# One engine per PSUM tile, and edge rows kept from chunk to chunk, in a recurrent transformer kernel

## The chip, the cores and the metric

The kernel runs on one core of a Trainium2 chip. The metric is the device time of one execution in microseconds (us). Engines are named as in the profile: PE is TensorE (PEld its weight loads), DVE is VectorE, ACT is ScalarE, POOL is GpSimd, SP is SyncE, which only issues DMAs here.

## What is computed

Two different blocks, A and B, are applied to a sequence of 2048 rows of 640 numbers, twice over. A is attention over segments of 32 rows with a recurrent memory of 8 rows: the memory that a segment writes is what the next one reads. B is a mixer: layer norm, w1, GELU, a shift of four column groups by one or two rows up or down, w2, a residual, layer norm, w3, GELU, w4, a residual.

```python
def _A_ref(x, mem0, Wq, Wk, Wv, Wo, seg_len):     # 32 heads of 192, M = 8 memory rows
    mem = mem0
    for s in range(n_seg):                        # 64 segments of 32 rows
        h = concatenate([mem, x[segment s]], axis=1)
        q, k, v = h @ Wq, h @ Wk, h @ Wv
        p = softmax(where(mask, q k^T * scale, -1e9))
        o = (p v) @ Wo
        mem = o[:, :M]; outs.append(o[:, M:])

def _B_ref(x, w1, w2, w3, w4):
    h = gelu(layernorm(x) @ w1)
    g0, g1 = h shifted by one row down, up        # column groups of 160
    g2, g3 = h shifted by two rows down, up
    x1 = x + concatenate([g0, g1, g2, g3]) @ w2
    return x1 + gelu(layernorm(x1) @ w3) @ w4

x = x + A(layernorm(x)); x = x + B(layernorm(x))
x = x + A(layernorm(x)); x = x + B(layernorm(x))
```

## The kernel before

**Steps and lanes.** The memory makes A a chain of 64 segments. The two passes over the sequence are run as two lanes, the second five segments behind the first (`LAG`), so that a step handles 40 rows (8 of memory, 32 of the segment) of each lane, 80 columns in all. There are 69 steps, `attention_step(t)`; in the first five and the last five only one lane is at work (40 columns, widened to 56 in matmuls). Activations are held transposed: `hT` has the 640 features in five groups of 128 partitions and the 80 rows as columns.

**Within a step.** The 32 heads are taken in eight groups of four. For each group, K and Q are made with 30 matmuls each into the PSUM tiles `psk` and `psq` (line L943). `psk` is copied to `kT` in three pieces: one by VectorE (L962), and two of 64 partitions (`fk2`, L969) by the engines that `K_ON` names, ScalarE and VectorE. `psq` goes to `qT` by ScalarE (L954). V is made for two groups at once with narrow matmuls (L999). Then the scores `pss` (L1059), a masked minimum on VectorE (L1071), Exp on ScalarE (`Pm`, L1078), sum, reciprocal and product on VectorE (L1082 to L1084), a transpose of P (`pst`, L1094), its copy `PT` by ScalarE (L1102), and PV (`pso`, L1111). `pso` is copied to `oT` in two halves, `HALVES`: columns of the first three chunks of features by VectorE (L1124), the other three by ScalarE (L1122). Each half is what one of two blocks of 15 Wo matmuls waits for (`project`, L1146); they add up in `psy` over all eight groups.

**The turn of a step.** When `psy` is complete, its memory columns go to the next step's `hT` (`fm`, L1173): one lane's by ScalarE, the other's by VectorE. The segment's columns go to `yTB` (`fy`, L1181), where two steps of two lanes make a chunk of 64 rows per lane, interleaved, 128 columns. All K and Q matmuls of the next step need `hT`.

**Chunks.** Every second step a chunk of the mixer is started, `chunk(c)` and `chunk_end(c)`, whose operations are spread over the steps after it; there are 34. `yTB` is transposed into `psx` and added to the residual rows in `xw`; layer norm twice (for the residual and for B's own norm); the result is transposed back (`psv`) into `vT`; w1, GELU, w2, w3, GELU, w4 follow. As the shift needs two rows beyond the chunk, and the rows beyond are not there when the chunk is taken, a chunk's rows begin two before and end two before a multiple of 64. The kernel of before keeps four more columns in `yTB` (copied to its front by GpSimd, `fh`, L1354) and computes two rows per lane ahead: a second transposition `psl` of 68 columns (`ftl`, L1339), their residual rows by small DMAs (L1307) into `lnx`, an addition (`fl`, L1348), and a layer norm together with 64 rows of x that a later segment of lane 0 will need (`f1` to `f3`, L1375 to L1395), transposed together into `psvl`. At the chunk's end its output is normed and transposed (`psn`, 128 columns), and ScalarE copies every second column to the `hT` of lane 1 (L1669).

**Order.** The program writes no order by hand. Each `add(engine, cost, due, fn, r=, w=, ...)` gives a planner an operation with an estimated cost. The planner simulates the engines, PSUM slots (pools A with six banks, B with two) and the DMA rate, and at each point takes, among the operations that can start within about 0.1 us, the one with the lowest rank. `RANK` is a table of ranks per kind of operation, found by a search; a function that has no entry uses its due time. Engines execute in the order that the planner wrote. The planner knows reads and writes of tiles, but not that two engines that read one PSUM tile are put one behind the other in the built program. Costs are formulas such as

```python
def mm_us(n, m=128, k=1):
    return k * (max(54, n) / 2400.0 + 0.0025)
def dve_us(n, ps_=True):
    return ((120 if ps_ else 58) + n) / 960.0 + 0.02
def act_us(n, ps_=True):
    return ((172 if ps_ else 224) + n) / 1200.0 + 0.02
```

In the last chunk (`last`), which runs alone, `vT` is copied from `psv` in two parts by ScalarE and VectorE (`halves`, L1403 to L1411), and extra matmuls (`warm`, L1262) are inserted.

Of the kernel before, what the change touches and what calls it, by code (L numbers as in the profile page):

```python
# [9 lines left out]
ACT = mybir.ActivationFunctionType  # L10
# [19 lines left out]
K_ON = ("ACT", "DVE")  # L30
# [14 lines left out]
HALVES = tuple(range(8))  # L45
# [24 lines left out]
        "apply_ln.f": (52.137, 88.961, 100.699,),  # L70
        "chunk.f1": (110.438,),
        "chunk.f2": (101.84,),
        "chunk.f3": (65.664,),
        "chunk.fe": (83.886,),
        "chunk.fe3": (46.088,),
        "chunk.fel": (32.784,),
        "chunk.fh": (42.145,),
        "chunk.fhr": (183.031,),
        "chunk.fhs": (122.734,),
        "chunk.fl": (118.876,),  # L80
        "chunk.fs": (46.206, 100.871,),
        "chunk.ft": (77.438,),
        "chunk.ftl": (91.661,),
        "chunk.fw": (82.421, 86.103, 82.645, 37.823, 49.706, 86.304, 87.341, 97.836, 107.843, 101.597, 117.412,
            27.174, 138.348,),
        "chunk.fx": (144.278,),
        "chunk.fx0": (48.1, 109.648,),
        "chunk.fxu": (68.848,),
        "chunk.fz": (125.444,),
        "gelu.f1": (108.489, 105.663, 99.941, 44.304, 104.272, 85.543, 44.936,),  # L90
        "gelu.f2": (104.016, 80.087, 147.301, 105.313, 115.841, 68.271, 102.092,),
        "gelu.f3": (81.071, 47.257, 92.576, 102.866, 16.713, 80.182, 169.139,),
        "gelu.f4": (108.795, 187.178, 115.889, 52.134, 39.445, 121.226, 162.103,),
        "ln_ops.f1": (113.498, 100.865,),
        "ln_ops.f2": (188.826, 114.703,),
        "load_b.fn": (113.282, 90.237, 183.209, 88.687, 76.718, 75.796, -6.492, 37.287, 74.679, 84.079, 105.79,
            81.564, 80.465,),
        "transposes.f": (91.19, 65.988, 82.894,),
    },
    "chunk_end": {  # L100
        "apply_ln.f": (92.741,),
        "chunk_end.fc": (101.233, 116.192, 33.171,),
        "chunk_end.fs": (152.914, 113.991,),
        "chunk_end.fst": (127.26, 114.197,),
        "chunk_end.fw": (130.447, 151.132, 77.606, 37.432, 151.624, 84.736,),
        "chunk_loads.f": (118.19, 79.814, 119.586, 65.5, 181.368,),
        "chunk_loads.fz": (149.036, 115.195,),
        "ln_ops.f1": (113.153,),
        "ln_ops.f2": (114.194,),
        "load_b.fn": (25.784, 148.908, 91.004, 157.492, 132.751, 85.692,),  # L110
        "transposes.f": (110.897,),
    },
    "first": {
        "attention_step.attend.f1": (53.315, 116.534, 97.712, 137.116, 129.596, 117.185, 54.167, 51.79,),
        "attention_step.attend.f2": (122.453, 33.318, 74.77, 70.523, 95.566, 89.213, 89.302, 101.992,),
        "attention_step.attend.f3": (109.938, 136.679, 76.042, 26.902, 123.564, 59.921, 70.35, 117.182,),
        "attention_step.attend.f4": (113.68, 87.629, 101.379, 78.084, 61.992, 103.186, 162.766, 48.64,),
        "attention_step.attend.f5": (95.973, 87.397, 115.074, 90.598, 74.249, 85.169, 62.671, 71.515,),
        "attention_step.attend.f6": (74.769, 118.85, 101.445, 53.2, 100.179, 38.5, 91.303, 65.688,),
        "attention_step.attend.f7": (79.267, 98.733, 127.69, 88.769, 101.401, 86.207, 109.807, 86.175, 59.4,  # L120
            81.845, 106.636, 89.216, 138.087, 76.712, 83.255, 93.735,),
        "attention_step.attend.fs": (109.158, 111.417, 121.159, 106.123, 129.223, 60.084, 111.282, 89.653,),
        "attention_step.fm": (48.96,),
        "attention_step.fy": (147.298,),
        "attention_step.keys_queries.fk": (102.585, 78.188, 99.287, 130.281, 111.901, 98.238, 91.544, 26.406,),
        "attention_step.keys_queries.fk2": (84.393, 163.652, 93.092, 97.448, 123.943, 130.917, 84.608, 126.811,
            33.999, 145.838, 116.093, 88.348, 115.075, 53.318, 85.162, 95.305,),
        "attention_step.keys_queries.fn": (73.475, 112.773, 95.166, 81.821, 50.11, 70.037, 127.367, 101.817, 75.07,
            118.539, 89.588, 129.858, 81.31, 37.249, 94.633, 31.69, 99.13, 89.248, 36.06, 43, 122.012, 21.413,
            131.651, 100.541, 130.892, 45.487, 83.907, 168.92, 120.166, 121.565, 73.851, 39.608, 11.881, 106.339,  # L130
            115.663, 145.027, 152.756, 51.785, 45.777, 72.891, 99.831, 94.353, 134.505, 126.888, 62.508, 125.75,
            96.816, 104.126, 77.632, 95.91, 83.98, 53.33, 164.127, 50.166, 143.384, 116.988, 76.705, 99.607,
            33.732, 135.249, 118.307, 103.713, 122.872, 102.021,),
        "attention_step.keys_queries.fq": (145.726, 101.991, 16.584, 72.383, 49.052, 59.527, 124.407, 97.897,),
        "attention_step.project.f8": (88.21, 86.563, 74.946, 49.461, 60.12, 72.038, 18.799, 146.753, 47.648,
            103.867, 75.726, 33.177, 92.295, 61.69, 78.374, 47.025,),
        "attention_step.v_copy.fe": (163.555, 108.338, 123.289, 107.631, 99.982, 161.514, 102.494, 73.06, 78.25,
            18.618, 96.542, 112.184, 117.386, 89.453, 136.682, 217.373,),
        "attention_step.values.fv": (101.461, 63.658, 11.217, 34.926, 41.032, 75.23, -20.798, 105.83,),
        "load_pair.fn": (78.644, 162.287, 19.053, 53.265, -8.243, 105.654, 67.504, 48.03, 96.854, 77.189, 77.899,  # L140
            62.364, 106.57, 59.689, 7.158, 41.956, 127.74, 35.31, 53.318, 105.363, 82.67, 134.583, 66.545, 128.724,
            14.499, 15.468, 128.738, -7.887, 139.922, 75.799, 72.889, 115.019, 78.308, 62.361,),
        "res_tile.fn": (40.422, 9.668, 106.558, 121.267, 17.862, 103.756, 27.246, -8.673, 66.049, 57.216, 92.25,
            57.768, 102.896, 73.672, 49.835, 81.724, 97.237, 67.576, 68.752, 86.302,),
    },
    "last": {
        "apply_ln.f": (92.911, 107.765, 92.908,),
        "chunk.fc2": (102.878, 64.939,),
        "chunk.fhr": (130.275,),
        "chunk.fs": (89.257, 122.931,),  # L150
        "chunk.ft": (107.248,),
        "chunk.fw": (121.032, 126.614, 122.007, 82.468, 128.297, 91.565, 52.504, 72.633, 103.673, 132.715, 79.925,),
        "chunk.fx": (74.485,),
        "chunk.fxu": (116.946,),
        "chunk.fz0": (164.135,),
        "chunk.halves.fa": (16.494, 117.489,),
# [1615 lines left out]
```

## Time and profile before

| | |
|---|---|
| median of three runs | 3290.59 us (3289.48 to 3293.75) |
| profiled execution | 3296.21 us, its span 3294.5 us |
| granted TensorE clock, mean | 0.991 |
| TensorE busy | 3178.7 us (96%) |
| VectorE, ScalarE, GpSimd busy | 2361.9, 1908.4, 235.5 us |
| HBM | 250 GB/s over the span |
| ScalarE's and VectorE's copies of oT (552 each) | 189.6 us (mean 344 ns) and 214.0 us (388 ns) |
| VectorE's and ScalarE's small copies of kT (552 each) | 174.3 us (316 ns) and 152.2 us (276 ns) |
| ScalarE's copy qT (552) | 290.9 us (mean 527 ns) |

The span is the time from the first to the last instruction of the profiled execution; the execution's own time is 1.7 us more. A row of a group has its line, engine, operation, what is written and read with its form (partitions x elements), the count, and then the busy time and the mean. A row of waits names the engine, tile and line that waited, what ended the wait, and the time in total, the number of times and the longest. A row of the timeline has the start, the duration, the engine and line, and in brackets the idle time before and what ended it. A row of a stretch has the busy time of PE, PEld, DVE, ACT and POOL, the granted clock, the DMA share and GB/s.

### The profile page before, as it was taken

Reading aid. Unit: us, or ns where it says so; the run is one execution under the profiler, and the core shown is the slowest. Engines: PE = TensorE matmul, PEld = TensorE weight load, DVE = VectorE, ACT = ScalarE, POOL = GpSimd, SP = SyncE. Lnnn points to the kernel's source line nnn. Section 1 sums busy time; section 2 is a strip of 40 time slices with the busy share of each in tenths; the row PEclk is TensorE's granted clock in tenths of the full one; section 3 lists DMA queues with packets and bytes.
Section 4 is the critical chain, followed back from the end, with each engine's and each line's share of the span. In section 5 each row is a group of like instructions: output and inputs, shape, how many; then the busy total and the mean of one; then the engine's idle time right before and its main releaser. Section 6 shows DMA issues by size and latency. Waiting matters only on the chain.

```text
span 3294.5 us, 173909 instructions
## 1 busy us (share of the span) xinstructions
PE 3178.7 (96%) x77339; PEld 2809.6 (85%) x77341; DVE 2361.9 (72%) x7320; ACT 1908.4 (58%) x4837; POOL 235.5 (7%) x483
## 2 busy tenths in 40 slices
PE   5899999999999999999999999999999999999997
PEld 4788888888888888888888888888888888888876
DVE  2576777777777777777777777777777777777665
ACT  2346566666565656666666666565666666666443
POOL 0000000000000000000000000000000000000000
PEclk7999999999999999999999999999999999999999
DMA  9787778777777877777778777777877777777886
GB/s 372 249 285 260 236 245 272 239 237 249 265 239 235 271 245 237 240 265 252 238 245 274 234 232 256 261 237 237 276 243 235 241 268 244 237 251 264 271 282 203
DMA packets 409753, 833.67 MB, mean 253 GB/s; under 512 B 39680, under 2 KB 207311, under 8 KB 409000
## 3 DMA queue, kind: packets, MB, share of 16 engines
q1 hardware_dynamic: 401704, 809.47, 73.2%
q0 software_dynamic: 7136, 13.00, 1.3%
q8 instruction: 605, 9.91, 1.2%
q14 instruction: 148, 1.21, 0.1%
q10 hardware_dynamic: 160, 0.08, 0.0%
HBM read 817.14 MB, written 5.24 MB: 250 GB/s over the span
## 4 chain that ended last, share of the span: by engine, by line
PE 89%; DMA 3%; DVE 3%; ACT 3%; issue 1%; SPq 0%; POOL 0%; ACTq 0%; POOLq 0%; DVEq 0%
PE psy L1146 17%; PE psk L943 17%; PE psq L943 16%; PE psv L999 15%; PE pso L1111 5%; PE pss L1059 4%; PE psh L1565 3%; PE y L1611 3%; PE pst L1094 3%; PE psv L1039 2%; PE psh L1443 1%; DMA wst<-in_A_Wq_dram 1%; PE hs L1502 1%; DMA wst<-in_A_Wk_dram 1%; DVE oT L1124 1%
## 5 line engine op out<-in xcount | busy, mean ns | idle before, releaser
L943 PEld LDWEIGHTS <-wst 128*128 128x128 bf16 x19872 | 820.6, 99 | 51.9 <-issue 28.0
L1146 PE MATMUL psy<-oT,wo 128*128 128x80 bf16 (+1 forms) x16560 | 703.1, 200 | 30.5 <-DVE oT L1124 12.3
L979 ACT CAST V<-psv 96x384 bf16<-96x384 f32 (+3 forms) x1264 | 583.5, 473 | 195.2 <-PE psv L999 117.9
L1146 PEld LDWEIGHTS <-wo 128*128 128x128 bf16 x16560 | 637.8, 99 | 68.9 <-issue 50.6
L943 PE MATMUL psq<-hT,wst 128*128 128x80 bf16 (+1 forms) x9936 | 533.0, 200 | 7.9 <-DMA wst<-in_A_Wq_dram 4.8
L943 PE MATMUL psk<-hT,wst 128*128 128x80 bf16 (+1 forms) x9936 | 514.3, 200 | 19.7 <-DVE hT L1173 14.9
L999 PEld LDWEIGHTS <-hT 128*32 128x32 bf16 (+1 forms) x11840 | 294.7, 96 | 160.4 <-issue 8.6
L1124 DVE CAST oT<-pso 128x240 bf16<-128x240 f32 (+1 forms) x552 | 214.0, 388 | 280.9 <-ACT oT L1122 241.5
L954 ACT CAST qT<-psq 128x480 bf16<-128x480 f32 (+1 forms) x552 | 290.9, 527 | 101.6 <-PE psq L943 65.9
L999 PE MATMUL psv<-wv,hT 128*32 128x384 bf16 x5920 | 344.2, 328 | 0.1
L999 PE MATMUL psv<-wst,hT 128*32 128x384 bf16 x5920 | 341.6, 326 | 0.0
L1078 ACT ACTIVATE Pm<-pss,sm 80x320 bf16<-80x320 f32 (+2 forms) x552 | 278.1, 504 | 109.4 <-DVE sm L1071 101.3
L1071 DVE CUSTOM_DVE_ANT_1 pss<-pss,mask 80x320 f32<-80x320 f32 (+2 forms) x552 | 258.5, 468 | 114.3 <-PE pss L1059 104.6
L1102 ACT COPY PT<-pst 80x320 bf16<-80x320 bf16 (+2 forms) x552 | 221.9, 402 | 202.6 <-PE pst L1094 193.4
L969 ACT CAST kT<-psk 64x160 bf16<-64x160 f32 (+1 forms) x552 | 152.2, 276 | 310.0 <-PE psk L943 124.6
L943 PE MATMUL psq<-hT,wq 128*128 128x80 bf16 (+1 forms) x6624 | 322.0, 200 | 6.7 <-DMA wq<-in_A_Wq_dram 5.0
L943 PE MATMUL psk<-hT,wk 128*128 128x80 bf16 (+1 forms) x6624 | 321.4, 200 | 0.6 <-ACT hT L1698 0.4
L1122 ACT CAST oT<-pso 128x240 bf16<-128x240 f32 (+1 forms) x552 | 189.6, 344 | 219.0 <-PE pso L1111 169.2
L962 DVE CAST kT<-psk 128x320 bf16<-128x320 f32 (+1 forms) x552 | 256.1, 464 | 57.9 <-PE psk L943 20.8
L1082 DVE TENSOR_REDUCE sm<-Pm 80x4 f32<-80x320 bf16 (+2 forms) x552 | 250.4, 454 | 60.2 <-ACT Pm L1078 52.4
L943 PEld LDWEIGHTS <-wk 128*128 128x128 bf16 x6624 | 267.5, 99 | 11.8 <-issue 11.7
L1084 DVE TENSOR_TENSOR Pm<-Pm,sm 80x320 bf16<-80x320 bf16 (+2 forms) x552 | 255.7, 463 | 29.7 <-DVE sm L1083 0.5
(140 smaller groups left out, 4192.9 us busy)
## 6 DMA issues: line engine op xcount, KB each, us to landing
wst<-in_A_Wk_dram SPq DMA_DIRECT2D x556, 384.0 KB, 4.7
wst<-in_A_Wq_dram SPq DMA_DIRECT2D x556, 384.0 KB, 4.8
wst<-in_A_Wv_dram SPq DMA_DIRECT2D x418, 384.0 KB, 4.9
wstB<-in_B_w_dram SPq DMA_DIRECT2D x495, 320.0 KB, 4.6
wstB<-in_B_w_dram SPq DMA_DIRECT2D x132, 160.0 KB, 4.3
wo<-in_A_Wo_dram SPq DMA_DIRECT2D x8, 960.0 KB, 13.2
wv<-in_A_Wv_dram SPq DMA_DIRECT2D x2, 1536.0 KB
xw<-in_A_x_dram POOLq DMA_DIRECT2D x31, 80.0 KB, 4.6
```

The lines of the kernel that those rows point to most:

```text
L943: nc.tensor.matmul(out=o[:, cc, 0:W], lhsT=wv(kc, GW * j + cc * P, GW * j + (cc + 1) * P), rhs=h[:, kc, cw:cw + W], start=begin(pq), stop= ...
L954: nc.scalar.copy(out=qT[:, :, c0:c0 + N], in_=T(pq)[:, :, off:off + N])
L962: nc.vector.tensor_copy(out=k4[:, :, 0::3, c0:c0 + N], in_=p4[:, :, 0::2, off:off + N])
L979: (nc.vector.tensor_copy if e == "DVE" else nc.scalar.copy)(out=v_part(*dst), in_=a_)
L999: nc.tensor.matmul(out=o[32 * u:32 * u + n3, :], lhsT=left[:, kc, 32 * g3:32 * g3 + n3], rhs=wv(kc, a, a + GWH), start=(kc == 0), stop=(kc ...
L1071: nc.vector.tensor_tensor_reduce(out=o, in0=o, in1=maskt.unsqueeze(1).to_broadcast([NR, HG, N]), scale=-scale, scalar=3.0e38, op0=ALU.add, ...
L1078: nc.scalar.activation(out=Pb[0:NR, :, 0:N], in_=o, func=ACT.Exp, bias=sm_[0:NR, 0:1], scale=-1.0)
L1082: nc.vector.tensor_reduce(out=sm_[0:NR, 2:2 + HG], in_=Pb[0:NR, :, 0:N], axis=AX.X, op=ALU.add)
L1084: nc.vector.tensor_tensor(out=Pb[0:NR, :, 0:N], in0=Pb[0:NR, :, 0:N], in1=sm_[0:NR, 6:6 + HG].unsqueeze(2).to_broadcast([NR, HG, N]), op=A ...
L1102: nc.scalar.copy(out=Pt[0:KV, :, 0:N], in_=T(pst)[0:KV, :, c0:c0 + N])
L1124: nc.vector.tensor_copy(out=o_[:, 0:3, off:off + N], in_=T(pso)[:, 0:3, 0:N])
L1146: nc.tensor.matmul(out=o[:, m, cw:cw + W], lhsT=wo[:, cc, m * P:(m + 1) * P], rhs=o_[:, cc, 0:W], start=st, stop=True, skip_group_check=True)
```

## The change

Every PSUM tile is now read by one engine. `oT` is one copy of six chunks by ScalarE, which both Wo blocks wait for. The three pieces of `kT` are all VectorE's. The memory columns of both lanes are one VectorE copy. In the last chunk the transposes go to two tiles, of three and two groups, each with one engine.

The mixer's look-ahead is gone: no `psl`, `fl`, `fh`, no look-ahead rows in `lnx`. `yTB` has 128 columns; the two last rows of an odd step are written to its front, so a chunk's 128 columns are 62 of its own rows per lane and, in its first four columns, the two rows per lane that come after it. These serve as the two rows beyond (`vT`'s last four columns are copied from `psv`'s first four), and GpSimd keeps them in `edge_x` (rows 96 to 99 of the V tiles) for the next chunk, which puts them back as its first rows and norms them again with the statistics of the chunk before (`st4[0]` and `st4[4]` by turns). The loads of residual rows take two rows of the coming chunk per lane. The output's transposition is a matmul by every second column of the identity, into an f32 tile of 64 columns. `RANK` has new numbers throughout.

```diff
-K_ON = ("ACT", "DVE")
+K_ON = ("DVE", "DVE")
-HALVES = tuple(range(8))
 RANK = {
...
-    Vt = [ctile([KR, 2 * VP], bf16, f"V{i}") for i in range(VT_BUFS)]
+    Vt = [ctile([P, 2 * VP], bf16, f"V{i}") for i in range(VT_BUFS)]
...
-    yTB = ctile([P, KC, XB + 4], bf16, "yTB")
+    yTB = ctile([P, KC, XB], bf16, "yTB")
...
-    lnx = h2u[0:TOK + 4, Dm:2 * Dm]
+    lnx = h2u[0:TOK, Dm:2 * Dm]
...
+    edge_x = [v_[96:100, 0:Dm] for v_ in Vt]
...
-            if p_ in HALVES:
-                for hf in range(2):
-                    def f7(op, hf=hf):
-                        if hf:
-                            nc.scalar.copy(out=o_[:, 3:6, off:off + N], in_=T(pso)[:, 3:6, 0:N])
-                        else:
-                            nc.vector.tensor_copy(out=o_[:, 0:3, off:off + N], in_=T(pso)[:, 0:3, 0:N])
...
+            def f7(op):
+                nc.scalar.copy(out=o_[:, :, off:off + N], in_=T(pso)[:, :, 0:N])
+            add("ACT", act_us(GC * N), hi - HI[0], f7, r=(pso,), w=(ok,))
...
-                add("PE", mm_us(W, k=3 * KC), due, f8, r=(wb, oks[hf]), a=(psy,), order=order)
+                add("PE", mm_us(W, k=3 * KC), due, f8, r=(wb, ok), a=(psy,), order=order)
...
-            for e_, l in zip(("ACT", "DVE"), take):
...
+        if len(take) == 2:
+            def fm(op):
+                v = hn[:, :, SEG:SEG + 2 * M].rearrange("p k (l m) -> p k l m", l=2)
+                o = T(psy)[:, :, SEG:SEG + 2 * M].rearrange("p k (l m) -> p k l m", l=2)
+                nc.vector.tensor_copy(out=v[:, :, ::-1, :], in_=o)
+            add("DVE", dve_us(2 * KC * M), due, fm, r=(psy,), w=[B("hT", (t + 1) % 4, "m", l) for l in take])
...
+                nc.vector.tensor_copy(out=yv[:, :, l if t < T_A - 1 else 0, t0:t0 + n0], in_=T(psy)[:, :, xc:xc + n0])
+                if n0 < SEG:
+                    nc.vector.tensor_copy(out=yv[:, :, l if t < T_A - 2 else 0, 0:2], in_=T(psy)[:, :, xc + n0:xc + SEG])
...
+            if not last and 0 <= w0 + TOK <= S - 2:
+                todo.append((lane, lane, w0 + TOK, 2))
...
-        if not last:
-            add("PE", mm_us(128, k=KC), D(0.06), ftl, r=(B("yTB", 0), B("yTB", 1)), w=(psl,))
...
-        if not last:
-            add("DVE", 0.48, D(0.06), fl, r=(psl,), w=(B("lnx", "l"),))
...
-        if not last:
-            add("POOL", 0.7, D(0.1), fh, r=(B("yTB", 1),), w=(B("yTB", "h"),))
...
+        own, other = (0, 4) if c % 2 == 0 else (4, 0)
...
+            def fk0(op):
+                nc.gpsimd.tensor_copy(out=edge_x[c % 2], in_=xw[0:4, :])
+            add("POOL", 1.2, D(0.08), fk0, r=(xk,), w=(B("edge", c % 2),))
...
+            def fk1(op):
+                nc.gpsimd.tensor_copy(out=xw[0:4, :], in_=edge_x[1 - c % 2])
+            add("POOL", 1.2, D(0.15), fk1, r=(B("edge", 1 - c % 2),), w=(xk,))
+            apply_ln(uw, xw, 4, st4[other], 0, uk, xk, B("st", other), D(0.16))
...
-            nc.scalar.copy(out=vT[:, :, XB:XB + 4], in_=T(psl2)[:, :, TOK:TOK + 4])
+            nc.scalar.copy(out=vT[:, :, XB:XB + 4], in_=T(ps2)[:, :, 0:4])
...
-            ps4 = ps(PB, [P, KC, XB], bf16, "psn")
-            transposes(ps4, vx2, XB, D(1.5), (vxk,))
+            ps4 = ps(PB, [P, KC, TOK], f32, "psn")
+
+            def ft4(op):
+                for m in range(KC):
+                    nc.tensor.matmul(out=T(ps4)[:, m, :], lhsT=vx2[:, m * P:(m + 1) * P], rhs=ident[:, 0::2],
+                                     start=(m == 0), stop=(m == KC - 1), skip_group_check=True)
+            add("PE", mm_us(TOK, k=KC), D(1.5), ft4, r=(vxk,), w=(ps4,))
...
-                nc.scalar.copy(out=hT[tt % 4][:, :, d0:d0 + b - a], in_=pv[:, :, 0, a:b])
+                nc.scalar.copy(out=hT[tt % 4][:, :, d0:d0 + b - a], in_=T(ps4)[:, :, a:b])
```

## Prediction

> **What bounds the kernel now.** I read the page's first lines first, then the busy time of a long stretch, then who waits for whom, and last the timeline around single waits.
>
> ```profile
> PE 3178.7 (96%) x77339; PEld 2809.6 (85%) x77341; DVE 2361.9 (72%) x7320; ACT 1908.4 (58%) x4837; POOL 235.5 (7%) x483
> ...
> PEclk7999999999999999999999999999999999999999
> ```
>
> TensorE is the bound: the clock is full after the first slice, and no other engine reaches 75%. The stretch from 300 to 3000 us is the steady part:
>
> ```profile
> 300.00:3000.00 2700.00, 2662.46 (x64648) 2372.57 (x64646) 2009.37 (x6139) 1655.17 (x4086) 196.80 (x397) 1.00 0.75 249
> ```
>
> 98.6% looks as if nothing were left, but a matmul's row lasts 0.2 us while the next one is issued long before: in the timeline 18 matmuls of 80 columns take 0.81 us and 6 take 0.38, so one is issued every 0.036 us. A pause of up to some 0.16 us in the issue is therefore covered by the row before it, and every idle time shown is some 0.16 us too short. So I counted. In this stretch the groups have 13596 matmuls for Wo and 27293 for Q and K at 0.036 us, 11380 narrow ones for V at 0.041 (16 in 0.83 us, 4 in 0.34), 2724 for the scores (a third of them with 160 columns, at 0.07), 5428 for the transposes of P and for PV at 0.036, 2405 for the mixer's wide ones at 0.056, 962 at 0.136, and 860 transposes, mostly at 0.056. The sum is about 2562 us. So about 138 of 2700 us (5%) is lost in the issue, not 38. Two kinds of saving exist: fewer matmuls, and shorter pauses.
>
> Who makes TensorE pause, and who makes the copying engines pause:
>
> ```profile
> PE psk L943 <- DVE hT L1173: 14.9, 29, 0.5
> PE psy L1146 <- DVE oT L1124: 12.3, 64, 0.7
> ...
> PE pso L1111 <- ACT PT L1102: 7.0, 39, 0.4
> ...
> PE pss L1059 <- DVE kT L962: 5.0, 6, 1.3
> ```
>
> ```profile
> DVE oT L1124 <- ACT oT L1122: 241.5, 234, 2.2
> ...
> DVE kT L969 <- ACT kT L969: 69.5, 134, 2.6
> ...
> DVE hT L1173 <- ACT hT L1173: 51.2, 58, 1.3
> ```
>
> The second list is the finding: wherever one PSUM tile is emptied by both engines, the second copy waits for the first. The split costs time instead of saving it, and 362 us of VectorE's queue stand still behind it. The timeline shows it for the output of a head group, and at the turn of a step:
>
> ```profile
> 1505.52 0.36 ACT L1122 CAST oT<-pso 128x240 bf16<-128x240 f32 x1 [1.05 <-PE pso L1111]
> ...
> 1505.91 0.41 DVE L1124 CAST oT<-pso 128x240 bf16<-128x240 f32 x1 [0.57 <-ACT oT L1122]
> ...
> 1537.04 0.19 ACT L1173 CAST hT<-psy 128x40 bf16<-128x40 f32 x1 [1.32 <-PE psy L1146]
> 1537.26 0.20 DVE L1173 CAST hT<-psy 128x40 bf16<-128x40 f32 x1 [1.11 <-ACT hT L1173]
> ...
> 1537.52 0.81 PE L943 MATMUL psk<-hT,wst 128*128 128x80 bf16 x18 [0.52 <-DVE hT L1173]
> ```
>
> **The change part by part.** The sum is made against the profiled execution, 3296.2 us (span 3294.5, and 1.7 around it); the median of the three runs, 3290.6, lies 5.6 lower.
>
> *Fewer matmuls.* The look-ahead transposes psl go: five in each of 33 chunks.
>
> ```profile
> 1539.51 0.45 PE L1339 MATMUL psl<-ident,yTB 128*68 128x128 bf16 x5
> ...
> 1539.79 0.38 PE L943 MATMUL psk<-hT,wst 128*128 128x80 bf16 x6
> ```
>
> The next group starts 0.28 us after them, so 33 x 0.28 = 9.2 us of pure issue. The five psn transposes of a chunk (0.28 us too) become matmuls with 64 moving columns, every second one of the identity; by the 80-column row (0.036) and the 68-column psvl I take 0.03 each, 0.15 a set, so 33 x 0.13 = 4.3 us. No row shows a moving operand read with a step; if it ran at half rate this saving would be 0, and I see no reason for a loss beyond that. The psvl set runs in 30 chunks instead of 33: 0.5 us. Sum 14.0, range 9.5 to 14. It is real time, since TensorE is the bound.
>
> *The turn of a step.* The next step's first K matmul waits for two copies in a row, 1537.04 to 1537.46. One VectorE copy of 128x80 takes their place; between its rows of 128x40 (0.200) and 128x160 (yTB, 0.342) that is about 0.25 us. So 0.17 us less at each of the 58 turns with two lanes, 9.9 us; only 29 of the waits are visible, which gives 4.9 as the low end. I take 8. The copy must find VectorE free: behind an operation of 0.49 us it would lose what it gains, and it has no second engine to fall back on; hence a low end of 0.
>
> *oT by ScalarE alone.* Before, 0.36 and 0.41 us one behind the other, 0.79 from the first start to the last end. After, one copy of 480 elements: the qT row has the same form (mean 0.527, 0.55 with two lanes). A group's whole output is ready 0.24 us earlier, its first half 0.14 to 0.19 later. Here the Trainium skill speaks against the change: TensorEngine Tiling (Array Packing), section PSUM Bottleneck, advises using ScalarE and VectorE both to empty PSUM. By that rule the halves would be done together in 0.41 us and the change would cost 0.14 x 552 groups = 77 us of latency. The trace says otherwise: the second half waits 241.5 us for the first engine, and another page, PSUM — Partial Sum Buffer, section on bank collisions, says why one would order them so: two engines reading one bank in the same partitions at once is an error that the hardware does not arbitrate. I go by the trace. TensorE's waits for VectorE's oT are 12.3 us in 64 times, with 0.16 for each 22.5. The first Wo block of a group now starts later than the first half allowed, so I take half, 12 us, with ends of 0 and 22.
>
> *kT by VectorE alone.* 0.49, 0.33 and 0.33 us on one queue, 1.15 us against 0.49, 0.28 and 0.33 with two hand-overs, about the same. Q's 30 matmuls (1.08 us) lie between K and the scores and hide it; TensorE waited six times in all. Taken as 0; without that cover 0.1 us x 552 = 55 us either way, which nothing in the trace suggests.
>
> *Load of the copying engines.* VectorE loses 214 us (oT), gains 552 x 0.316 = 174 (kT), loses fl's 16, gains 33 applications on four rows (0.44 each, 15) and the strips of the last two rows of yTB (64 x 0.17, 11): about 30 less. ScalarE gains 290 - 190 = 100 (oT) and loses 152 (kT) and 13 (hT): 65 less. More counts that VectorE no longer stands still for ScalarE 362 us, nor ScalarE for VectorE 118 (87.1 on kT, 30.5 on oT), with softmax steps queued behind. What TensorE waits for there is PT, 7.0 us in 39 times, with 0.16 each 13.2, and Pm, 2.8 us in five times: I take a third of the 17, 6 us, ends 0 and 12. ScalarE's queue has a longer piece now: a PT copy (0.40) or Exp that comes just after an oT copy starts waits up to 0.19 us more.
>
> *Mixer edges.* GpSimd gets two copies of 4x640 per chunk (fk0, fk1) and loses fh (128x20, 0.19) and the look-ahead loads; it issues five loads a chunk as before, since two-row loads now go into xw. They wait, as the main ones, for the last reader of xw (row L1626). The loads of L1307, ahead of which GpSimd stood 1288 us, are gone; nobody waited for those. No row shows the copy; the memset of 4x640 took 0.62 us, the planner charges 1.2. The power operation of the layer norm can be queued behind fk0, and the row-4 application waits for fk1, but uw is needed only after w1, the GELU and w2. A second rule bears on this: SBUF — State Buffer, section on the two separate sides, says that GpSimd and VectorE share a port pair, held for a whole instruction against VectorE operations in a two-port mode or with two SBUF inputs. By it 66 copies of 0.62 to 1.2 us could hold VectorE up by 41 to 79 us; no row here shows such a delay. VectorE is idle a quarter of the time, so I take 0 for TensorE and keep 20 us (0.6 a chunk, if each hit a turn or a softmax) as the far end.
>
> *Tail and one-lane steps.* At 3268.4 ScalarE 0.48, VectorE 0.29 and ScalarE 0.18 run in a row before psh; from two banks they run side by side, 0.65 instead of 1.12, and a part of it again at 3281: 0.6 us. The one-lane steps from 3072 on lose 4 us each of 48 even in the visible rows; shorter chains may give 2.
>
> *New order.* Every due rank is changed, so which block fills which pause is drawn anew. That can't be costed; it counts in both directions in the range.
>
> Sum: 14 + 8 + 12 + 6 + 2.6 = 42.6. 3296.2 - 42.6 = 3253.6 for a profiled execution, 3248 for the median.
>
> **The rivals.** (A) *Only the work counts*: pauses are moved, not shortened, because TensorE then waits for PT or Pm instead. For it: softmax is a chain over ScalarE and VectorE with every link already in the list of waits. Against: the turn of the step has nothing behind it but that copy. 14 + 2 us: 3275. (B) *Slower, by the late first half*: the order puts Wo close behind PV, and TensorE waits for ScalarE's one long copy, 0.14 us beyond what the first half allowed before. With turn, work and tail still gaining 24.6, this decides from 24.6 / 0.14 = 176 of the 552 groups on; with 350 of them it is 49 us, so 3315. Against: before, with a latency of 0.79, only some 71 visible waits of 552 were for oT. (C) *More is won*: an order found with copies that take what the planner thinks (it planned both halves at once) halves the 138 us: 69 + 14 + 3 = 86, so 3205. (D) The edit turns out empty, for example because all was hidden: 3290; the psl rows make this unlikely.
>
> **How the numbers follow.** About 0.2% (6.6 us) is what a measurement can tell from no change. Forecast 0.45, own range 3228 to 3272; A 0.22; C 0.14; B 0.15; D 0.04. Faster 0.45 + 0.22 + 0.14 less a little of A's edge: 0.80; same 0.05; slower 0.15. The range leaves out B and the lower part of C: 3200 to 3288.
>
> **What would show it.** After: no psl rows and psn at half its issue; no wait of a copy for the other engine's copy of the same tile; psk waiting about 0.35 instead of 0.52 at a turn; fewer waits of psy for oT; VectorE some 30 and ScalarE some 65 us less busy. More than 150 psy waits for ScalarE's oT would show B; new PT and Pm waits of the old total A. A longer span with fewer pauses at turns would make the account by steps wrong and point to the order.

## The result, and the profile after

The changed kernel takes 3265.19 us (median of four runs) against 3292.17 for the kernel before in the same set: a ratio of 0.9912, 95% interval 0.9888 to 0.9936. In a second set, with more runs of before beside it, the ratio was 0.9913 (0.9897 to 0.9930), 3263.21 against 3293.58. So the change is worth 27 to 30 us, 0.9% (the intervals reach from 21 to 37 us). The forecast was 42.6 us less, 3248; the measured time lies inside the stated range.

The page's engine line and the granted clock, and a stretch of the steady part (busy PE, PEld, DVE, ACT, POOL, clock, DMA share, GB/s):

```profile
PE 3149.0 (96%) x77161; PEld 2790.2 (85%) x77161; DVE 2285.5 (70%) x7377; ACT 1854.6 (57%) x4217; POOL 269.6 (8%) x510
...
PEclk8999999999999999999999999999999999999999
```

```profile
300.00:2970.00 2670.00, 2638.09 (x64463) 2357.43 (x64466) 1939.93 (x6181) 1610.89 (x3570) 227.84 (x424) 1.00 0.75 251
```

TensorE is still the bound, at 98.8% of the stretch by its rows and a full clock. It has 178 matmuls fewer than before. By this line VectorE has 76 us less to do and ScalarE 54 (30 and 65 were expected), GpSimd 34 more. The line counts rows that overlap once; with all durations added up, VectorE has 33 us less, near the expected 30, and ScalarE 58. TensorE's waits now (in total, times, longest):

```profile
PE psx L1202 <- DVE vbg L1192: 9.7, 1, 9.7
PE psk L928 <- DVE hT L1149: 9.6, 29, 0.3
...
PE psq L928 <- DMA wst<-in_A_Wq_dram: 8.6, 16, 1.1
...
PE pst L1079 <- DVE Pm L1069: 5.2, 7, 1.5
...
PE psy L1122 <- ACT oT L1104: 4.3, 11, 0.5
...
PE pso L1096 <- ACT PT L1087: 3.1, 11, 0.5
...
PE pss L1044 <- DVE kT L947: 1.7, 3, 0.9
```

The turn of the step fell from 14.9 to 9.6 us, oT from 13.9 (12.3 for VectorE's half, 1.6 for ScalarE's) to 4.3, PT from 7.0 to 3.1. What came in their place stands in the same list: weights that land late, 8.6 us in 16 times against 4.8 in 8, and Pm, 5.2 against 2.8. The first row is one wait in the first 15 us of the run; it was 3.4 us before. The list of VectorE's waits has no copy of an oT, kT or hT tile by ScalarE any more; its longest is the wait for TensorE itself (`DVE hT L1149 <- PE psy L1122`, 160.0 us). A turn in the timeline (start, duration, engine, line), with one copy in place of two in a row:

```profile
1529.10 0.24 DVE L1149 CAST hT<-psy 128x80 bf16<-128x80 f32 x1 [3.83 <-PE psy L1122]
...
1529.39 1.02 PE L928 MATMUL psk<-hT,wst 128*128 128x80 bf16 x24 [0.33 <-DVE hT L1149]
```

The wait is 0.33 us where it was 0.52. From step 6 to step 63 only every second turn looks like this. At the others a block of the mixer stands between Wo and K, here in the kernel before, so that no idle time shows:

```profile
1586.48 0.72 PE L1565 MATMUL psh<-hTB,wstB 128*128 128x128 bf16 x10
1587.16 1.02 PE L943 MATMUL psk<-hT,wst 128*128 128x80 bf16 x24
```

The output's transposition with the stepped identity:

```profile
1517.20 0.31 PE L1631 MATMUL psn<-ident,h2u 128*128 128x64 bf16 x5
1517.35 0.38 PE L928 MATMUL psk<-hT,wst 128*128 128x80 bf16 x6
```

The next group starts 0.15 us after it, so a moving operand read with a step of two is issued at the full rate, 0.03 us for 64 columns.

One delay is new. GpSimd's copies of the edge rows hold up VectorE's `stash` copy (rows of V put by for later, bf16, from SBUF to SBUF) when the two meet:

```profile
310.99 0.71 POOL L1351 COPY xw<-V 4x640 bf16<-4x640 bf16 x1 [2.95 <-DVE h2u L1192]
...
311.15 0.82 DVE L1007 COPY stash<-V 32x384 bf16<-32x384 bf16 x2 [0.30 <-ACT V L964]
```

The first of these two VectorE copies took 0.65 us, ending 0.11 us after GpSimd's. In the profile 29 of the 464 `stash` copies meet a copy into `xw`, and these 29 took 0.66 us each where the others took 0.25: 12 us in all. No engine is listed as waiting for them.

**An account of TensorE's issue.** Matmul rows hide short pauses, as the prediction says, so I made the same sum for every run: from the first matmul of a group to the first of the next, less the group's issue time (columns / 2.4 ns and 2.5 ns for each matmul, as in the planner's formula, which gives the 0.036 us of the rows for 80 columns; 0.040 us for a narrow V matmul), where more than 0.06 us is left, put down to what released it. It is taken from the first K matmul of step 6 to that of step 63, the part with two lanes. "Switch" is the time lost on going into the narrow V matmuls and out of them. Going in costs 0.096 us. Going out shows as 0.14 or 0.15 us, but four narrow matmuls follow four others by 0.1625 us and not by 0.160; with that, 0.106 us remain, and 46 of the 55.8 us. Each row is one profile. The two profiles of the changed kernel (after, after2) differ by 6.3 us in length, so differences of a few us between two lengths tell nothing by themselves.

| us, in the stretch | length | switch | oT | turn | PT | Pm | kT | weights |
|---|---|---|---|---|---|---|---|---|
| before | 2713.0 | 55.8 | 28.8 | 22.5 | 12.2 | 3.4 | - | 3.0 |
| b_oT | 2709.0 | 55.7 | 26.0 | 22.5 | 17.4 | 0.5 | - | 5.7 |
| b_turn | 2708.6 | 56.4 | 28.9 | 13.9 | 11.3 | 2.8 | - | 2.2 |
| b_copies | 2695.4 | 53.5 | 28.5 | 13.9 | 1.1 | 10.0 | - | 3.1 |
| b_pework | 2703.0 | 55.3 | 29.1 | 22.5 | 12.2 | 2.8 | - | 2.3 |
| b_all | 2683.4 | 52.7 | 28.5 | 13.9 | - | 5.1 | 9.6 | 3.4 |
| after | 2684.3 | 58.8 | 11.2 | 13.9 | 6.8 | 0.8 | - | 13.6 |
| after2 | 2678.0 | 61.5 | 11.2 | 13.9 | 6.8 | 0.3 | - | 7.7 |
| a_split | 2738.2 | 53.3 | 44.4 | 13.9 | 19.5 | 2.9 | 23.9 | 4.9 |

The whole gain of the profiled pair lies in this stretch, 28.7 us: 12.2 us less issue time (2572.3 and 2560.1) and 16.5 us less lost (140.7 and 124.2). The start, up to step 6, is 1.4 us longer than before, and the end from step 63 on is as long (279.7 and 279.5 us).

### The profile page after: what moved, and what is told of

Same layout as the page of the kernel before. It is cut to its first block, busy times and chain, and to the rows that moved or that the text cites. A ratio compares the mean times of both kernels' runs of the same rounds, so it can differ in the third digit from the quotient of the medians.

```text
span 3266.9 us, 172868 instructions
## 1 busy us (share of the span) xinstructions
PE 3149.0 (96%) x77161; PEld 2790.2 (85%) x77161; DVE 2285.5 (70%) x7377; ACT 1854.6 (57%) x4217; POOL 269.6 (8%) x510
## 4 chain that ended last, share of the span: by engine, by line
PE 88%; DMA 7%; issue 2%; DVE 2%; ACT 1%; SPq 0%; POOL 0%; POOLq 0%; ACTq 0%; DVEq 0%
PE psq L928 16%; PE psy L1122 16%; PE psk L928 16%; PE psv L984 15%; PE pss L1044 5%; PE pso L1096 5%; PE psh L1531 3%; DMA wst<-in_A_Wq_dram 3%; PE y L1577 3%; PE pst L1079 2%; DMA wst<-in_A_Wk_dram 2%; PE psv L1024 2%; PE psh L1409 1%; PE hs L1468 1%; DMA wst<-in_A_Wv_dram 1%
## 5 line engine op out<-in xcount | busy, mean ns | idle before, releaser
L928 PEld LDWEIGHTS <-wst 128*128 128x128 bf16 x19872 | 803.7, 99 | 64.1 <-issue 35.7
L1122 PE MATMUL psy<-oT,wo 128*128 128x80 bf16 (+1 forms) x16560 | 703.6, 200 | 26.4 <-issue 8.6
L964 ACT CAST V<-psv 96x384 bf16<-96x384 f32 (+3 forms) x1264 | 595.9, 474 | 168.3 <-PE psv L984 102.4
L1122 PEld LDWEIGHTS <-wo 128*128 128x128 bf16 x16560 | 630.8, 99 | 51.2 <-issue 35.1
L928 PE MATMUL psq<-hT,wst 128*128 128x80 bf16 (+1 forms) x9936 | 518.0, 200 | 13.7 <-DMA wst<-in_A_Wq_dram 8.6
L928 PE MATMUL psk<-hT,wst 128*128 128x80 bf16 (+1 forms) x9936 | 508.6, 200 | 17.7 <-DVE hT L1149 9.6
L1104 ACT CAST oT<-pso 128x480 bf16<-128x480 f32 (+1 forms) x552 | 293.7, 532 | 264.0 <-PE pso L1096 238.9
L954 DVE CAST kT<-psk 64x160 bf16<-64x160 f32 (+1 forms) x1104 | 340.4, 308 | 131.3 <-PE psk L928 62.6
L984 PE MATMUL psv<-wst,hT 128*32 128x384 bf16 (+1 forms) x5920 | 343.3, 326 | 2.2 <-issue 1.1
L928 PEld LDWEIGHTS <-wk 128*128 128x128 bf16 x6624 | 270.8, 99 | 17.6 <-issue 13.9
L928 PEld LDWEIGHTS <-wq 128*128 128x128 bf16 x6624 | 267.4, 99 | 6.5 <-DMA wq<-in_A_Wq_dram 3.0
## 6 DMA issues: line engine op xcount, KB each, us to landing
wo<-in_A_Wo_dram SPq DMA_DIRECT2D x8, 960.0 KB, 12.3
```

What stands on the lines that cost most here:

```text
L928: nc.tensor.matmul(out=o[:, cc, 0:W], lhsT=wv(kc, GW * j + cc * P, GW * j + (cc + 1) * P), rhs=h[:, kc, cw:cw + W], start=begin(pq), stop= ...
L954: copy(out=k4[r0:r1, :, jj, c0:c0 + N], in_=p4[r0:r1, :, 1, off:off + N])
L964: (nc.vector.tensor_copy if e == "DVE" else nc.scalar.copy)(out=v_part(*dst), in_=a_)
L984: nc.tensor.matmul(out=o[32 * u:32 * u + n3, :], lhsT=left[:, kc, 32 * g3:32 * g3 + n3], rhs=wv(kc, a, a + GWH), start=(kc == 0), stop=(kc ...
L1104: nc.scalar.copy(out=o_[:, :, off:off + N], in_=T(pso)[:, :, 0:N])
L1122: nc.tensor.matmul(out=o[:, m, cw:cw + W], lhsT=wo[:, cc, m * P:(m + 1) * P], rhs=o_[:, cc, 0:W], start=st, stop=True, skip_group_check=True)
```

## The experiments

The theories: (1) a PSUM tile that two engines empty makes TensorE pause, and issue time is real time, so the parts have their worth in any order and add up; (2) what a part is worth is decided by the order around it; (3) two engines empty a tile faster than one. All edits but those of the ranks keep each engine's order of instructions; only the edited ones differ. Ratios are to the kernel before, timed beside them.

**b_oT**: oT whole by ScalarE, in the kernel before.

```diff
+                both_ = []
...
-                        if hf:
-                            nc.scalar.copy(out=o_[:, 3:6, off:off + N], in_=T(pso)[:, 3:6, 0:N])
-                        else:
-                            nc.vector.tensor_copy(out=o_[:, 0:3, off:off + N], in_=T(pso)[:, 0:3, 0:N])
+                        if not both_:
+                            nc.scalar.copy(out=o_[:, :, off:off + N], in_=T(pso)[:, :, 0:N])
+                        both_.append(op)
```

> The kernel before, in its own order of instructions on every engine, with one edit: each oT tile is copied whole by ScalarE (at the place of the first of its two half copies), VectorE's half is gone. Theory 1 (a PSUM tile emptied by two engines makes TensorE pause, whatever the order): 12 to 18 us less than before, TensorE's waits for oT fall from 14 us to under 7, and VectorE's wait for ScalarE's oT copy (241.5 us) is gone. Theory 2 (the gain comes from the new order, the old order has the pauses built in): under 4 us less, the waits for PT or Pm grow by what those for oT lose. Theory 3 (two engines are better than one): slower by up to 20 us, more psy waits for ScalarE's oT.

Measured: 3287.63 against 3290.82, ratio 0.9991 (0.9980 to 1.0002). The waits of TensorE in its profile:

```profile
PE pso L1111 <- ACT PT L1102: 10.3, 58, 0.4
...
PE psy L1146 <- ACT oT L1123: 5.3, 15, 1.0
```

The visible waits for oT fall from 13.9 us to 5.3, but in the account they are 26.0 us in 168 times where there were 28.8 in 139: short waits, since the first Wo block now needs the whole copy. And PT comes later, behind the longer copy on ScalarE's queue: 10.3 us visible against 7.0. Where a PT copy comes just after an oT copy, it starts more than 0.1 us after its transposes have ended in 69 of 138 cases, before in 8 of 109. Theory 1 had its 12 to 18 us here and got at most 6.6 (the interval's end). It fails for this part, in this order; theory 3 fails too. What theory 2 said (under 4 us, PT later) is what came.

**b_turn**: one VectorE copy for the memory columns of both lanes, in the kernel before.

```diff
+            both_ = []
...
+                    if len(take) == 2:
+                        if not both_:
...
+                            nc.vector.tensor_copy(out=v[:, :, ::-1, :], in_=o)
+                        both_.append(op)
+                        return
```

> The kernel before, in its own order, with one edit: at a turn with two lanes the memory columns of both lanes are copied by one VectorE instruction instead of ScalarE and then VectorE. Theory 1: 8 to 10 us less; the visible wait at a turn falls from 0.52 us to about 0.33. Theory 2: under 3 us. Theory 3: no gain, since VectorE comes late to it (slower by up to 5 us).

Measured: 3284.13 against 3290.82, ratio 0.9977 (0.9969 to 0.9986), 4.6 to 10.2 us. The wait at the turn:

```profile
PE psk L943 <- DVE hT L1177: 9.6, 29, 0.3
```

It was 14.9, 29, 0.5. Theory 1 holds for the wait itself: the account's turn goes from 22.5 to 13.9 us. At 28 turns with nothing between Wo and K, 0.68 us of lost issue becomes 0.50; at 29 with a block of the mixer between, 0.12 us becomes nothing. How much of the 8.6 us the kernel gets is less sure. By the medians it is 6.7; the stretch is 4.4 us shorter, as waits before Q and K matmuls grew by 4, which is within what two profiles of one kernel differ by.

**b_copies**: both of these, and all pieces of kT by VectorE.

```diff
-copy = nc.vector.tensor_copy if K_ON[jj - 1] == "DVE" else nc.scalar.copy
+copy = nc.vector.tensor_copy
```

> The kernel before, in its own order, with all three copy edits: oT whole by ScalarE, memory columns of both lanes in one VectorE copy, all three pieces of kT by VectorE. Theory 1: the two gains add up, 20 to 28 us less, kT adding nothing. Theory 2: under 7 us less. If kT counts, this lies more than 5 us away from the sum of the other two runs.

Measured: 3278.11 against 3290.82, ratio 0.9961 (0.9949 to 0.9974), 12.7 us. That lies between what theories 1 and 2 allowed (20 to 28, under 7). The sum of the two runs before is 9.9, so kT's part is 2.8 by the medians; by the stretch it is 9.2 (17.7 against 4.1 and 4.4). No run has the kT edit alone, so its part stays open. By the account PT's waits are gone (1.1 us of 12.2) and Pm's have come up (10.0 of 3.4): taking ScalarE out of kT helps ScalarE's softmax step and hurts VectorE's.

**b_pework**: less work for TensorE, copies split as before. VectorE's addition after psl is left out too (not shown), so the look-ahead rows lack the attention's output.

```diff
-            for m in range(KC):
-                nc.tensor.transpose(out=o[0:TOK + 4, m, :], in_=yTB[:, m, XB - TOK:XB + 4], identity=ident[:, :])
...
-            transposes(ps4, vx2, XB, D(1.5), (vxk,))
...
+                for m in range(KC):
+                    nc.tensor.matmul(out=T(ps4)[:, m, :], lhsT=vx2[:, m * P:(m + 1) * P], rhs=ident[:, 0::2],
+                                     start=(m == 0), stop=(m == KC - 1), skip_group_check=True)
```

> The kernel before, in its own order, with only TensorE's work cut: the look-ahead transposes psl and the addition after them are left out (so the look-ahead rows lack the attention's output), and the output's transposition has 64 moving columns, every second one of the identity, instead of 128. The copies stay split over two engines. Theory 1 (issue time is real time): 13.5 us less, of which 9.2 from psl and 4.3 from the 64 columns; the next group starts 0.15 us after the first psn matmul instead of 0.28. Theory 2 (pauses absorb it): under 5 us less. If the stepped operand is read at half rate: 9 us less and psn still takes 0.28.

Measured: 3284.04 against 3290.82, ratio 0.9983 (0.9972 to 0.9993), so 2 to 9 us, less than expected. In the steady stretch, with 29 of the 33 chunks, it is 10.1 us shorter, of 11.9 that 0.41 us a chunk would give. The two readings don't agree, so the cost was put to the test the other way round.

**b_psl4**: every psl transpose four times.

```diff
-            for m in range(KC):
+            for m in [m_ for m_ in range(KC) for _ in range(4)]:
                 nc.tensor.transpose(out=o[0:TOK + 4, m, :]
```

> The kernel before, in its own order, with every psl transpose issued four times instead of once: 15 more matmuls of 128 columns in each of 33 chunks, at 0.056 us 27.7 us in all. Theory 1 (issue time is real time): 24 to 30 us slower than before, so that psl itself was worth 8 to 10. Theory 2 (pauses absorb half of it, as the 6.8 us for an expected 13.5 of the run with the cut work suggest): 10 to 18 us slower.

Measured: 3317.54 against 3293.01, 24.5 us more, ratio 1.0079 (1.0054 to 1.0103). One block in the timeline:

```profile
1549.83 1.28 PE L1339 MATMUL psl<-ident,yTB 128*68 128x128 bf16 x20
1550.94 0.38 PE L943 MATMUL psk<-hT,wst 128*128 128x80 bf16 x6
```

1.11 us to the next group, four times 0.28. The steady stretch is 23.0 us longer, of 24.4 for 29 chunks. So some nine tenths of issue time is run time (the interval allows 18 to 34 us of the 27.7); by this, psl is worth 8 us or a little more, and the cut work as a whole, as an estimate, some 12. Theory 1 holds for TensorE's work. Why b_pework got less, with an interval that ends at 9 us, is not explained.

**b_all**: b_copies and b_pework together, in the order of the kernel before (the edits are those of the runs before). The changed kernel's copies and second norms of the edge rows and its last chunk are not in it.

> The kernel before, in its own order, with the three copy edits and the cut TensorE work together (psl and the addition after it left out, so the look-ahead rows lack the attention's output; psn with 64 columns). Apart from the order and the edge rows' bookkeeping this is the changed kernel. Copies alone gave 12.7 us and the cut work 6.8 by the medians. Theory 1 (parts add, the new order is worth nothing by itself): 24 to 29 us less than before, level with the changed kernel within 4 us. Theory 2 (the order has to be searched for whole copies): 17 to 21 us less, 6 to 10 us behind the changed kernel, with psy's waits for ScalarE's oT still above 25 us in all.

Measured: 3267.14 against 3293.58, 26.4 us less, ratio 0.9924 (0.9909 to 0.9938). It is level with the changed kernel, 3.9 us behind by the medians of the same set, with overlapping intervals. The single parts by medians add up to 12.7 + 6.8 = 19.5, by the steady stretch to 17.7 + 10.1 = 27.8 (b_all: 29.6). Theory 1 holds for the whole: these edits without a new order give nearly all of the gain.

**after2**: the changed kernel in the same set.

> The changed kernel once more, on the same chip as the others of this set: 25 to 31 us less than before.

Measured: 3263.21, 30.4 us less. In the account the new order has 17 us less in waits for oT than b_all (11.2 and 28.5) and none for kT, but more at switches, in waits for PT and for weights. It exchanges waits; the net of order and edge rows together is those 4 us or nothing.

**a_split**: oT in two halves again, in the changed kernel and its order.

```diff
-                nc.scalar.copy(out=o_[:, :, off:off + N], in_=T(pso)[:, :, 0:N])
+                nc.vector.tensor_copy(out=o_[:, 0:3, off:off + N], in_=T(pso)[:, 0:3, 0:N])
+                nc.scalar.copy(out=o_[:, 3:6, off:off + N], in_=T(pso)[:, 3:6, 0:N])
```

> The changed kernel, its order kept, with one edit: at the place of ScalarE's whole oT copy, VectorE copies the first half and ScalarE the second. Theory 1: the second copy waits for the first, the output is ready some 0.25 us later and both Wo blocks wait for it: 8 to 20 us slower than the changed kernel, VectorE's and ScalarE's waits for each other's oT come back. Theory 2 (in any order other work covers it): within 4 us of the changed kernel.

Measured: 3332.13, 68.9 us more than the changed kernel of the same set and 38.6 more than before (ratio to before 1.0118, 1.0103 to 1.0133). ScalarE's longest wait, and TensorE's:

```profile
ACT oT L1105 <- DVE oT L1104: 596.6, 549, 4.0
```

```profile
PE psy L1123 <- DVE oT L1104: 28.5, 48, 1.0
PE pso L1096 <- ACT PT L1087: 12.5, 40, 0.6
PE pss L1044 <- DVE kT L947: 11.0, 31, 0.9
```

ScalarE stands behind VectorE's half nearly every time (549 of 552), up to 4 us, and then PT and kT are late as well. In an order made for one copy, a split costs over three times the most that was expected (20), against the 3.2 us that joining the halves gained in the old order. In the old order the second copy found the other one at work less often: VectorE waited for ScalarE's half in 234 cases of 552 (241.5 us), ScalarE for VectorE's in 90 (30.5 us). So the wait comes with the split in both orders, and its price does not. But the 68.9 us are not the price of that wait alone: VectorE has 214 us more work, in places that no plan made for it, and stood 131.1 us waiting for `pso` there (21.0 us in the kernel before). No run takes these apart.

**a_oldrank**: the changed kernel, planned with the old table of ranks.

> The changed kernel with the table of ranks of the kernel before (functions that are new fall back on their due times), so the planner writes another order. Theory 1 (order worth nothing by itself): within 5 us of the changed kernel. Theory 2 (the search found 10 us or more for this set of operations): 10 to 40 us slower than the changed kernel, so that most of the gain is gone.

Measured: 3433.53, 170 us more than the changed kernel, ratio to before 1.0426 (1.0411 to 1.0442).

```profile
PE psy L1132 <- ACT oT L1114: 39.3, 83, 0.9
PE pso L1106 <- ACT PT L1097: 25.5, 65, 0.6
PE psh L1541 <- DVE h2u L1243: 18.7, 29, 0.7
PE pst L1089 <- DVE Pm L1079: 17.5, 38, 1.8
```

No theory had so much. A table of ranks that fits one set of operations is worth little for another: of the some 206 us that the new table gives over an empty one (a_norank, below), the old one gives 36 (by medians of different sets). Several links of the softmax chain are late. So "order searched anew" was no extra: planned with the old table, the edits make the kernel 140 us slower than before. Only the old order kept as it was, as in b_all, does without.

**b_norank** and **a_norank**: both kernels with an empty table, so in the order of due times.

> The kernel before with an empty table of ranks, so that the planner orders by due times. To be compared with the next run. 50 to 200 us slower than before.

> The changed kernel with an empty table of ranks. Theory 1 (the edits are worth their 25 us in any order): 20 to 40 us less than the kernel before with an empty table. Theory 2 (what an edit is worth depends on the order as much as on the edit): the difference lies outside of 10 to 50 us, on either side.

Measured: 3578.69 for the kernel before and 3469.19 for the changed one, ratios to before 1.0870 (1.0846 to 1.0895) and 1.0539 (1.0515 to 1.0563). The empty table costs the kernel before 286 us, more than the 50 to 200 expected. The change is worth 109.5 us there, 3.1%, outside of what theory 1 allowed. TensorE's waits for oT in the two profiles, before and after:

```profile
PE psy L837 <- DVE oT L815: 101.9, 139, 0.9
```

```profile
PE psy L823 <- ACT oT L805: 68.9, 98, 1.3
```

They fall by 33 us, but that is not where the difference lies. From step 6 to step 63 the two take 2950.7 and 2866.3 us, 84.4 apart (the whole spans 115.5). The changed kernel has 11.7 us less to issue there. What TensorE loses at full clock is the same in both, 276.8 and 276.1 us: while waits for oT got shorter, others got longer (for PT, visible, from 43.5 to 56.4). The other 72 us are lost while the granted clock is at half. In the kernel before that is the case for 215.7 us of the stretch, in 39 spells, in the changed one for 61.4 us, in 15; they cost 102.5 and 30.4 us beyond the issue time at full clock, waits within them included. A stretch of both, before first (the last three numbers are granted clock, DMA share, GB/s):

```profile
1000.00:2000.00 1000.00, 940.13 (x22028) 838.26 (x22025) 673.30 (x2082) 561.88 (x1392) 68.01 (x138) 0.96 0.69 230
```

```profile
1000.00:2000.00 1000.00, 944.71 (x22622) 838.13 (x22623) 674.95 (x2169) 564.50 (x1255) 78.08 (x145) 0.99 0.71 235
```

So what the change is worth beyond its usual gain comes, in this stretch, from time at half clock and not from fewer waits at full clock. Why the clock falls less often, with equal losses at full clock, no run shows.

**a_nopace**: the changed kernel without the dependencies that hold weight loads back.

```diff
-        elif o.paced:
+        elif False:
```

> The changed kernel, its order kept, without the dependencies that hold the weight loads back to the planner's times; a load then starts when its buffer is free. Theory 1 (TensorE now waits for weights because the steps are shorter than the pace allows): 4 to 10 us less than the changed kernel, TensorE's waits for wst, wstB and wq nearly gone. Theory 2 (the buffers or the rate of the DMAs set it): within 4 us of the changed kernel, the waits stay.

Measured: 3380.84, ratio to before 1.0258 (1.0230 to 1.0285), some 114 to 118 us more than the changed kernel, which was timed in other sets. Both theories are wrong. The loads of K and Q weights on the page (count, KB, median us from issue to landing), first the changed kernel, then this one:

```profile
wst<-in_A_Wk_dram SPq DMA_DIRECT2D x556, 384.0 KB, 4.9
wst<-in_A_Wq_dram SPq DMA_DIRECT2D x556, 384.0 KB, 5.0
```

```profile
wst<-in_A_Wk_dram SPq DMA_DIRECT2D x556, 384.0 KB, 6.9
wst<-in_A_Wq_dram SPq DMA_DIRECT2D x556, 384.0 KB, 7.4
```

And TensorE's waits, of which these were 5.3 and 5.1 us in the changed kernel:

```profile
PE psq L928 <- issue: 31.4, 31, 2.4
PE psk L928 <- issue: 31.4, 33, 2.4
```

A load takes 2 us longer when it may start as soon as its buffer is free. That loads in flight together share the rate, so that the one needed first lands later, would fit, but no run shows which loads met. Without the pace the kernel loses some 115 us; whether a slightly looser one would remove the late weights of the changed kernel was not tried.

## Why the prediction came out as it did

**What bounds it**: right. TensorE's issue is the bound, and an added matmul costs its issue time to nine tenths (b_psl4). The sum of 2562 us does not come from the rates as printed, which give 2577, but from unrounded ones (80 / 2.4 ns and 2.5 ns for 80 columns); over the same 2700 us the trace gives 2559 us of issue and 141 lost, where the prediction had 138.

**Fewer matmuls, 14.0**: right in kind, a little too large. The stepped operand runs at the full rate, psn's next group starts 0.15 us after it as assumed, and psl is worth 8 us rather than 9.2. Alone, the cut work gave 6.8 us by the medians (2 to 9) and 10.1 of 11.9 in the stretch; together with the copies (b_all) it fits the larger number.

**The turn, 8**: right in kind and size. 6.7 us by b_turn (4.6 to 10.2); the copy took 0.242 us where 0.25 was interpolated, and it did find VectorE free. That only 29 of the waits were visible has a reason that the prediction did not see: at every second turn a block of the mixer fills most of the wait, so the turn does have something behind it but that copy.

**oT by ScalarE alone, 12**: this term failed. Alone and in the old order it gave 3 us (b_oT, at most 6.6). The prediction took half of the waits for VectorE's oT as gone; instead the later first half made new short waits, 26.0 us where there were 28.8, and ScalarE's queue brought PT later. That is rival B's mechanism, at a size that only cancelled the gain. The new order did cut these waits, to 11.2 us, more than the 12 forecast, but paid with others: 3 to 6 us more at switches and 5 to 11 for weights.

**PT and Pm, 6**: half right. PT fell from 12.2 to 6.8 us and Pm from 3.4 to below 1, 8 us together. But weights came late in their stead, 13.6 and 7.7 us in two executions against 3.0. The prediction never asked what shorter steps would make late next on the DMA side.

**kT, 0**: not settled. By the medians the edit adds 2.8 us, by the stretch 9.2, and with it PT's waits go from 17.4 (b_oT) to 1.1 us while Pm's go from 0.5 to 10.0.

**Mixer edges, 0**: right for TensorE, in whose list no wait for them stands. GpSimd's 66 copies took 0.711 us each, near the memset's row and not the planner's 1.2. The delay of VectorE that the prediction weighed is there, but at 12 us (29 `stash` copies, 0.41 us more each) and not 41 to 79: fewer than half of the copies met a VectorE copy of this kind.

**Tail and one-lane steps, 2.6**: the tail's 0.6 is there, since the last chunk, from its first transpose to the end, takes 29.6 us where it took 30.4. The 2 us of the one-lane steps are not: from step 63 on, tail included, the kernel is 0.2 us shorter. The profiles of the kernel before with other edits have 275.1 to 280.1 us there, so 2 us could not have been told.

**The new order, not costed**: worth 4 us or nothing on top of the edits (b_all, which lacks the edge rows' copies), but needed as soon as the planner is run again on the changed operations (a_oldrank).

So 42.6 came down to 27 to 30. By the single runs some 9 are missing on oT, 2 on the one-lane steps and 2 to 4 on the work, and late weights stand against the gain in PT; this is a reckoning from runs in the old order, and no run adds these parts up. The measured time lies nearer to rival A (3275) than to the forecast (3248), and A's mechanism, that waits move, is what happened to oT, though they moved to weights and switches rather than to PT and Pm. That the largest copying term failed and the time still lies in the range (3228 to 3272) is partly luck, owed to the range's width. The advice of the Trainium skill that the prediction decided against (TensorEngine Tiling (Array Packing), section PSUM Bottleneck), to empty PSUM with ScalarE and VectorE both, does not hold in this trace for two halves of one tile: VectorE's half waited 241.5 us for ScalarE's, and joining the halves was level or better (3287.63 against 3290.82 in the old order).

## What to carry to other kernels

When two engines empty one PSUM tile here, the second waits for the first, and it is the list of an engine's waits for the other engine that shows it; but the split's price is what waits behind it in that order, so compare edits with the order held fixed, one at a time. A wait that little else can fill (the turn of a recurrence) gave back most of what was cut from it; a wait within a dense schedule mostly moved. When a change is worth more in one order than in another, look at the granted clock before the waits. A table found by search belongs to its set of operations: after an edit of the operations, either keep the old order of instructions or search again.

## What the runs showed of the hardware that I had not expected

Going into the narrow matmuls of 32 columns costs TensorE 0.096 us, and leaving them 0.106 beyond the 0.1625 us of the last four. At 228 changes each way in 57 steps that is 46 us, the largest single loss in the account, and one that the change leaves as it is.

A copy of four rows by GpSimd held up a bf16 copy from SBUF to SBUF by VectorE until it had ended (0.66 us where 0.25 is usual, 29 times). VectorE's copies of `psk` from PSUM that met such a copy were not slower (0.24 and 0.31 us, against 0.24 and 0.32).

Weight loads that start as early as buffers allow landed 2 us later (6.9 and 7.4 against 4.9 and 5.0), and the kernel was some 115 us slower.

The granted clock stayed full in the stretch of kernels that lose 124 to 178 us of issue there (after, before, a_split). With more lost at full clock it fell to half for 20 us (a_nopace, 209 us lost), 48 us (a_oldrank, 243), 61 us (a_norank, 276) and 216 us (b_norank, 277). The last two show that the sum of the losses does not decide it.
